# Whole-row first loads, a thinned third routing and re-placed weight splits in an attention and mixture-of-experts kernel

## The chip, the cores and the metric

The kernel runs on one core of one Trainium2 chip. The metric is device time in microseconds for one execution; lower is better. A core has TensorE (PE in the rows; PEld is its weight load), VectorE (DVE), ScalarE (ACT), GpSimd (POOL) and SyncE (SP), each with its own instruction queue that runs in order, and 16 DMA engines that all queues feed. Here SP and ACT issue the plain transfers (queues q1 and q10), GpSimd the gathers.

## The reference

Three stages follow each other; everything is float32.

```
q_pool = q.reshape(B, H, S//2, 2, D).mean(axis=3)          # B=4, H=8, S=1152, D=64
attn   = softmax(q_pool @ k.T / sqrt(D)) @ v               # 576 pooled queries per head
x      = attn.transpose(0,2,1,3).reshape(2304, 512)
logits = x @ w_gate + modality_bias[modality_id]           # 8 experts
e      = argmax(logits);  gate = softmax(logits)[e]
x      = gate * (relu(x @ w1[e]) @ w2[e])                  # top-1 expert per row
logits = x @ phi                                           # 32 slots, 4 for each of 8 experts
slots  = softmax(logits, axis=0).T @ x
out    = softmax(logits, axis=1) @ ffn_e(slots)            # a second expert network on the slots
```

## The kernel before

Attention works on 16 **pairs** of heads, p = 0 to 15; four pairs make a batch. A pair has 36 **positions** `pos`: two halves u of the queries, nine blocks c of 128 keys, two heads j. At each position PE computes a 128x288 block of scores by two matmuls (`S1` L247 and `S2` L253, on values cut into high and low parts), and ACT takes the exponential of it (`e`, L257). After every sixth position, at pos 2, 8, 14, 20, 26 and 32, stands a `group`: 12 matmuls with V (`PV`, L267), and three additions into the running sum of exponentials (`accadd`, L278 and L280, on GpSimd; in pair 15 mostly on DVE). There are three score buffers in PSUM.

Between these stands the work of other pairs. `maxpiece` (L198, L195): matmuls into `mps` whose row maximum DVE takes (L200), for the pair after this one; PSUM has three buffers for it, shared with everything small (tag `mx`). `maxred` (into `MXZ`, L207 and L209) and `maxrow` (`nps` on PE, then L218 and L221 on DVE) end it, at pos 29 and 31. `prep` (casts `KC`, `QC` on ACT, `KL`, `QL` by subtraction, copies by SP's queue) makes the operands of pair p+2. `fin0`, `fin1`, `fin2` finish a half: sums and routing logits (`sg`, `sgT`, `xr`).

When a batch is done, its **routing** is put into `queue` at pos 18 of the next pair, as a list of one-instruction steps, and the loop over positions takes one from its head: at every second position for p < 12, at every position from p = 12 on (`QSTEP`, L653). The steps are `choose` (L380 to L385: maximum and chosen expert), `gates` (L409 to L414), `place` (`ranks`: small matmuls `rp` L352 to L356; then L389 to L393; then one-hot rows, four ACT instructions (L368, L369) at a time at the groups; then `table` L362) and `count`. Routing of batches 0, 1 and 2 thus starts in pairs 4, 8 and 12. With the third batch (p = 12) there is more: `ahead.select` picks the expert of a first task of the expert stage, `fetch` gathers its weights (eight gathers into tiles that attention no longer needs), `split` cuts them into high and low parts (a cast on ACT L750, a subtraction on DVE L751), `load_x` gathers its rows, and `turn` transposes them. The list `work` holds what is placed by position; `AF2`, `5 * i + 3` and the numbers after `p == n - 1` set it. For p = 16 the fourth routing and the first matmuls of the expert stage (`hp`, L759 to L761) run.

The first pair has its own code (`first`). It needs each head's K and Q twice, on partitions 0 to 63 and 64 to 127. `twice` loads each piece by two transfers of 64 partitions: 12 from SP, 6 from ACT. A transfer waits for the landing of the one eight before it, since eight completion semaphores take turns; so ACT's fourth, fifth and sixth transfers hold ACT itself. Then come `khi` (cast, L472), `klo` (subtraction, L476), `qadd` (L465, L466), 18 maximum pieces, `maxred`, two subtractions of pair 1's `prep` (L173), and `maxrow0` (L229, L236, L241), which the first `S2` waits for.

Of the kernel before, what the change touches and what calls it, by code (L numbers as in the profile page):

```python
# [7 lines left out]
F32 = mybir.dt.float32  # L8
F32R = mybir.dt.float32r
I32 = mybir.dt.int32  # L10
AF = mybir.ActivationFunctionType
# [5 lines left out]
B, H, S, D = 4, 8, 1152, 64  # L17
HP = H // 2
SQ = S // 2
# [19 lines left out]
QSTEP = 2  # L39
# [42 lines left out]
def attention(ctx, tc, g):  # L82
    nc = tc.nc
    qT, kT, vT, wg = g["qT"], g["kT"], g["vT"], g["wg"]
# [6 lines left out]
    V = nc.vector  # L91
# [20 lines left out]
    n = len(pairs)  # L112
# [89 lines left out]
    def maxred(p, blks):  # L202
        s = st[p]
        Z = MXZ
        if min(blks) < 4:
            b0, b1 = min(blks), min(max(blks), 3) + 1
            V.reduce_max(Z[:, :, 64 + b0:64 + b1], s["mxp"][:, 0:8].rearrange("p (j b) t -> p j b t", j=2)[:, :, b0:b1], axis=AX.X)  # L207
        if 4 in blks:
            V.reduce_max(Z[:, :, 68:69], s["mxp"][:, 8:9].unsqueeze(1).to_broadcast([128, 2, 1, 3]), axis=AX.X)  # L209
# [207 lines left out]

    def in_order(r, select=None):
        choose, place, count, gates = r
        if select is None:  # L420
            return choose[:3] + gates + choose[3:] + place + count
        expert, rows = select
        place = place[:1] + count + expert + [lambda i=i: ahead.fetch(i) for i in range(2)] + place[1:]
        return choose[:3] + gates + choose[3:] + place + rows

    def first():

        b, hp = pairs[0]
        st[0] = s = dict(v=VT[0], mxp=sp.tile([128, 9, 3], F32, name="mxp"))
        operands(0)  # L430
        kx = [VT[i].rearrange("p a b c -> p (a b c)") for i in (2, 3)]
        qx = cp.tile([128, 2, 2, SQ], F32, name="qx0", tag="xr", bufs=1)
        third = lambda t: slice(t * 384, (t + 1) * 384)
        qq = [slice(0, 128), slice(128, 384)]
        q2 = [slice(0, 384), slice(384, SQ)]
        js = lambda j: slice(j * 64, (j + 1) * 64)

        def twice(eng, out, src):

            for u in range(2):  # L440
                eng.dma_start(out=out[u * 64:(u + 1) * 64], in_=src)

        twice(nc.sync, kx[0][:, third(0)], kT[b, hp, js(0), third(0)])
        for c in (qq[0], slice(128, SQ)):
            twice(nc.scalar, qx[:, 0, :, c], qT[b, hp, js(0), :, c])
        for t in (1, 2):
            twice(nc.sync, kx[0][:, third(t)], kT[b, hp, js(0), third(t)])
        twice(nc.scalar, qx[:, 1], qT[b, hp, js(1)])
        for t in range(3):
            twice(nc.sync, kx[1][:, third(t)], kT[b, hp, js(1), third(t)])  # L450
        load(1)
        load_v(0)
        P = nc.gpsimd
        P.memset(mask[64:69], 0.0)
        P.affine_select(out=mask[64:69], in_=mask[64:69], pattern=[[-1, 5], [0, 128]],
                        compare_op=ALU.not_equal, fill=-1.0, base=0, channel_multiplier=1)
        P.memset(MXZ, 0.0)
        QB0 = s["QB"] = cp.tile([128, 2, 128], F32R, name="QB0", tag="rA", bufs=1)
        P.memset(QB0.bitcast(F32), 0.0)
        P.memset(QB.bitcast(F32), 0.0)  # L460
        V.memset(KH[0][64:69].bitcast(F32), 1.0)
        qs0 = cp.tile([128, 2, SQ], F32, name="qs0", tag="rR", bufs=1)

        def qadd(ve, j, c):
            ve.tensor_add(qs0[:, j, c], qx[:, j, 0, c], qx[:, j, 1, c])  # L465
            nc.scalar.copy(QS[0][:, j, c], qs0[:, j, c])  # L466

        def ql(ve, j, c):
            ve.tensor_sub(QL[0][0:64, j, c], qs0[0:64, j, c], QS[0][0:64, j, c].bitcast(F32))  # L469

        def khi(j, t):
            nc.scalar.copy(KS[0][:, j, third(t)], kx[j][:, third(t)])  # L472

        def klo(ve, j, t):
            c = third(t)
            ve.tensor_sub(KS[0][64:128, j, c], kx[j][64:128, c], KS[0][64:128, j, c].bitcast(F32))  # L476

        wp = ps.tile([128, 512], F32, name="warm", tag="pv", bufs=2)

        def warm(k):  # L480
            for _ in range(k):
                nc.tensor.matmul(wp[:, 0:128], ident, ident, start=True, stop=True)

        warm(SWARM[0])
        khi(0, 0)
        klo(V, 0, 0)
        qadd(V, 0, qq[0])
        khi(0, 1)
        qadd(V, 0, qq[1])
        khi(0, 2)  # L490
        maxpiece(0, 0)
        klo(V, 0, 1)
        maxpiece(0, 1)
        maxpiece(0, 2)
        klo(V, 0, 2)
        for i in range(3):
            khi(1, i)
        for m in range(3, 9):
            maxpiece(0, m)
            warm(SWARM[1])  # L500
        klo(P, 1, 0)
        qadd(P, 1, qq[0])
        qadd(P, 1, qq[1])
        klo(P, 1, 1)
        klo(P, 1, 2)
        for j in range(2):
            nc.scalar.copy(KH[0][0:64, j], kx[j][0:64])
        prep1 = prep(1, P)
        for j in range(2):
            ql(P, j, q2[0])  # L510
        load(2)
        for f in prep1[:4]:
            f()
        for j in range(2):
            qadd(P, j, q2[1])
            nc.scalar.copy(QB0[:, j, j * 64:(j + 1) * 64], qs0[:, j, 512:576])
            ql(P, j, q2[1])
        return prep1, warm
# [7 lines left out]
    for m in range(9, NP0):  # L526
        maxpiece(0, m)
        warm(SWARM[2])
    maxred(0, [0, 1, 2])
    for f in prep1[4:6]:  # L530
        f()
    maxrow0(0, [(0, 256), (256, 288)])
    nc.sync.dma_start(out=wgbd[0:64, :, 0:E], in_=wg[0])
    nc.sync.dma_start(out=wgbd[64:128, :, E:2 * E], in_=wg[1])
    consts = g["route_consts"]()
# [1 line left out]
    for p in range(n + 1):  # L537
        work = {}

        def at(pos, *fs):  # L540
            work[pos] = work.get(pos, []) + list(fs)
# [21 lines left out]
        if p < n:  # L563
            if p + 1 < n:
                late = 3 if p == 0 else 0
                at(MR[0] + late, lambda: maxred(p + 1, [0, 1, 2, 3, 4]))
                at(MR[1] + late, lambda: maxrow(p + 1))
            late = 4 if p == 0 else 0
            at(FA[0] + late, lambda: fin0(p, 0))
            at(FA[1] + late, lambda: fin1(p, 0))  # L570
            if pairs[p][1]:
                at(FA[2], lambda: fin2(p, 0))
# [10 lines left out]
        if p == n - 2:  # L583
            for i in range(2, 6):
                at(AF2[i - 2], lambda i=i: ahead.fetch(i))
            for i in range(6):
                at(5 * i + 3, lambda i=i: ahead.split(i))
        if p == n - 1:
            at(0, lambda: ahead.fetch(6), lambda: ahead.load_x(0), lambda: ahead.load_x(1))
            at(10, lambda: ahead.turn(0))  # L590
            at(12, lambda: ahead.turn(1))
            at(13, ahead.gates, lambda: ahead.fetch(7))
            for i in range(6):
                at(5 * i + 3, lambda i=i: ahead.split(6 + i))
        if p == n:
            group(n - 1, 2 * NKB // GS - 1)
            assert not queue
# [47 lines left out]
        for pos, z in enumerate(units):  # L645
            if pos >= 3:
                S1(p, *z)
            S2(p, *z)
            for f in work.get(pos, []):
                f()  # L650
            if p and pos % CST == 0 and consts:
                consts.pop(0)()
            if queue and pos >= (8 if p < n - 3 else 0) and pos % (QSTEP if p < n - HP else 1) == 0 and callable(queue[0]):  # L653
                queue.pop(0)()
            if pos % (2 * GS) == LAG - 1:
                for _ in range(NHOT):
                    if queue and not callable(queue[0]):
                        queue.pop(0)[1]()
            if pos == LAG - 1 and p > 0:
                group(p - 1, 2 * NKB // GS - 1)  # L660
            elif pos >= 2 * GS and pos % (2 * GS) == LAG - 1:
                group(p, pos // (2 * GS) - 1)
            if pos == 3 and p + 3 < n:
                if p == 0:
                    load_v(2)
                load(p + 3)
# [734 lines left out]
            f()  # L1401


def moe_kernel(tc, qT, kT, vT, wg, mod, mbias, w1, w2, phi, m2w1, m2w2, out):
    nc = tc.nc
    with ExitStack() as ctx:
        gp = ctx.enter_context(tc.tile_pool(name="gp", bufs=1))
# [3 lines left out]
        keep = {**dict.fromkeys(("ident", "ones128", "si", "sel", "xidx", "axidx", "nop"), gp),  # L1411
                **dict.fromkeys(("widx", "xidx", "ntask", "C", "agt", "awidx", "neg", "acc", "sums", "nm", "lT", "m4", "nmc", "w", "siw", "rc"), gf)}
        dr = ctx.enter_context(tc.tile_pool(name="dr", bufs=1, space=DRAM))
        g = dict(qT=qT, kT=kT, vT=vT, wg=wg, w1=w1, w2=w2, phi=phi, m2w1=m2w1, m2w2=m2w2, out=out)
        g["xs"] = dr.tile([PAD + N, XW], F32, name="xs")
        g["ls"] = dr.tile([PAD + N, NSL], F32, name="ls")

# [169 lines left out]
def _layout(inputs):  # L1587
# [4 lines left out]
    a = {}  # L1592
# [10 lines left out]
    w2 = inputs["moe2_w2"].reshape(2, 4, KF, 128, DM)  # L1603
    parts = [w2[..., d0:d0 + dw].reshape(2, 4, KF * dw // 512, 512 // dw, 128, dw).transpose(0, 2, 4, 3, 1, 5).reshape(-1, 128, 2048) for d0, dw in PARTS]
    a["m2w2"] = np.concatenate(parts)
    return a


# [18 lines left out]
```

## Time and profile before

| | |
|---|---|
| median of 3 runs | 847.51 us (847.25 to 848.96) |
| profiled execution | 850.42 us, span 848.7 us from its first to its last instruction |
| PE, share of the span busy | 95% (804.7 us) |
| DVE, ACT, POOL | 68%, 55%, 63% |
| mean granted TensorE clock | 0.988 of full speed |
| attention, from the first S1 (22.76 us) to the first matmul of the expert stage | 494.8 us |

The profiled execution is one more run than the three. PE is busy nearly throughout, so what counts is where it is not, and where its clock is below full speed. A row of the timeline gives start, duration, engine, line, operation, `out<-in`, count, and in brackets how long the engine sat idle before and what ended that. A row of a stretch gives its bounds and length, then busy time (and count) of PE, PEld, DVE, ACT and POOL, the granted TensorE clock as a share of full speed (1.00 is 2.4 GHz, 0.50 is 1.2 GHz), the share of the DMA engines busy, and GB/s.

### The profile page before, as it was taken

How to read it: one execution, taken by the hardware profiler on the slowest of the kernel's cores; microseconds unless marked ns; L12 is line 12 of the kernel's file. 1: busy time of each engine (PE TensorE's matmuls, PEld its weight loads, DVE VectorE, ACT ScalarE, POOL GpSimd, SP SyncE). 2: the span in 40 equal slices, each digit the busy share in tenths (PEclk: the TensorE clock that was granted, in tenths of full speed). 3: DMA queues.
4: the chain of work that ended last, by engine and by line, in shares of the span. 5: the costliest groups of instructions: out<-in, count | busy, mean ns of one | idle time of the engine just before them, and what ended most of it. 6: DMA issues, size and time to landing. Idle time of an engine off the chain costs nothing. (4 is left out here: it accounts for less than half of the span.)

```text
span 848.7 us, 16170 instructions
## 1 busy us (share of the span) xinstructions
PE 804.7 (95%) x5808; PEld 616.1 (73%) x5808; DVE 576.0 (68%) x1180; ACT 465.1 (55%) x1106; POOL 537.3 (63%) x497
## 2 busy tenths in 40 slices
PE   4889999999999999999899999999999999999997
PEld 3657777677677676777676667788898988888446
DVE  5777777768776877877686765666576665764262
ACT  4446665657766568665377573355465555553123
POOL 5768899998888987789598842634545454441100
PEclk9999999999999999999799999999999999999999
DMA  8896649675664595566362210787786876847797
GB/s 262 199 242 154 174 137 225 144 196 145 152 168 139 120 241 151 140 159 167 99 149 79 70 57 1 220 287 252 251 288 196 312 275 248 275 160 255 277 398 225
DMA packets 58874, 163.13 MB, mean 192 GB/s; under 512 B 14682, under 2 KB 23322, under 8 KB 54682
## 3 DMA queue, kind: packets, MB, share of 16 engines
q1 hardware_dynamic: 41844, 96.42, 40.8%
q0 software_dynamic: 13760, 47.60, 16.7%
q10 hardware_dynamic: 3184, 18.02, 6.0%
q8 instruction: 47, 0.77, 0.4%
q14 instruction: 39, 0.32, 0.1%
HBM read 110.71 MB, written 10.90 MB: 143 GB/s over the span
## 5 line engine op out<-in xcount | busy, mean ns | idle before, releaser
L280 POOL TENSOR_TENSOR acc<-acc,e 128x576 f32<-128x576 f32 x214 | 313.6, 1465 | 39.7 <-ACT e L257 26.5
L257 ACT ACTIVATE e<-sc 128x288 f32<-128x288 f32 x576 | 224.2, 410 | 154.4 <-PE sc L253 132.3
L200 DVE TENSOR_REDUCE mxp<-mps 128x1 f32<-128x384 f32 x432 | 220.4, 549 | 102.2 <-PE mps L198 92.8
L247 PE MATMUL sc<-QS,KS 128*128 128x288 f32 x576 | 188.0, 334 | 4.2 <-ACT e L257 4.0
L253 PE MATMUL sc<-QL,KH 69*128 69x288 f32 x576 | 170.4, 298 | 2.2 <-DVE QL L241 1.7
L267 PE MATMUL pv<-e,V 128*64 128x288 f32 x1152 | 164.0, 421 | 0.0
L247 PEld LDWEIGHTS sc<-QS,KS 128*128 128x128 f32 x576 | 109.9, 191 | 53.9 <-issue 28.9
L198 PE MATMUL mps<-KS,QS 128*128 128x384 f32 x384 | 134.2, 354 | 13.6 <-ACT QS L466 11.2
L729 POOL DMA_INDIRECT wraw<-in_w,widx x72 | 72.9, 1012 | 108.6 <-DVE wlo L751 91.0
L267 PEld LDWEIGHTS pv<-e,V 128*64 128x64 f32 x1152 | 75.3, 138 | 64.3 <-issue 27.2
L751 DVE TENSOR_TENSOR wlo<-wraw,whi 128x512 fp32r<-128x512 f32 x144 | 95.4, 687 | 25.5 <-ACT whi L750 22.7
L253 PEld LDWEIGHTS sc<-QL,KH 69*128 69x128 f32 x576 | 109.9, 191 | 2.6 <-POOL QL L469 1.9
L750 ACT CAST whi<-wraw 128x512 fp32r<-128x512 f32 x144 | 83.9, 618 | 16.1 <-DMA wraw<-in_w,widx 11.6
L198 PEld LDWEIGHTS mps<-KS,QS 128*128 128x128 f32 x384 | 74.0, 194 | 16.8 <-ACT QS L466 11.7
L760 PE MATMUL hp<-xl,whi 128*128 128x256 f32 x288 | 80.8, 281 | 1.4 <-DVE xl L746 1.4
L759 PE MATMUL hp<-xh,whi 128*128 128x256 f32 x288 | 81.8, 284 | 0.0
L761 PE MATMUL hp<-xh,wlo 128*128 128x256 f32 x288 | 80.5, 280 | 0.0
L278 POOL TENSOR_TENSOR acc<-e 128x576 f32<-128x576 f32 x31 | 44.3, 1427 | 42.5 <-ACT e L257 42.4
L766 ACT ACTIVATE hh<-hp 128x256 fp32r<-128x256 f32 x72 | 27.6, 383 | 78.3 <-PE hp L761 65.6
L767 DVE SCALAR_TENSOR_TENSOR hl<-hp,hh 128x256 fp32r<-128x256 f32 x72 | 30.5, 423 | 44.5 <-ACT hh L766 27.2
L773 PE MATMUL yp<-whi,hh 128*128 128x512 f32 x144 | 59.6, 414 | 0.0
L760 PEld LDWEIGHTS hp<-xl,whi 128*128 128x128 f32 x288 | 54.1, 188 | 4.9 <-DVE xl L746 2.2
(363 smaller groups left out, 1243.7 us busy)
## 6 DMA issues: line engine op xcount, KB each, us to landing
mw<-in_m2w ACTq DMA_DIRECT2D x16, 1024.0 KB
mw<-in_m2w SPq DMA_DIRECT2D x16, 1024.0 KB
V<-in_vT SPq DMA_DIRECT2D x16, 576.0 KB
KX<-in_kT SPq DMA_DIRECT2D x15, 576.0 KB
QX<-in_qT SPq DMA_DIRECT2D x15, 576.0 KB
KS<-KC SPq DMA_DIRECT2D x30, 288.0 KB
KH<-KC SPq DMA_DIRECT2D x30, 288.0 KB
QS<-QC SPq DMA_DIRECT2D x60, 144.0 KB
```

Source lines behind the costliest of these rows:

```text
L198: nc.tensor.matmul(mps[:, :384], s["QS"][:, j, blk * 128:(blk + 1) * 128], s["KS"][:, j, ks], start=True, stop=True)
L200: V.reduce_max(s["mxp"][:, slot, t:t + 1], mps[:, :384], axis=AX.X)
L247: nc.tensor.matmul(sc[:, :NU], s["KS"][:, j, c * 128:(c + 1) * 128], s["QS"][:, j, u * NU:(u + 1) * NU], start=True, stop=False)
L253: nc.tensor.matmul(sc[:, :NU], s["KH"][0:69, j, c * 128:(c + 1) * 128], s["QL"][0:69, j, u * NU:(u + 1) * NU], start=False, stop=True)
L257: nc.scalar.activation(s["e", u, c][:, j], sc[:, :NU], AF.Exp, scale=SM)
L267: nc.tensor.matmul(pv[j * 64:(j + 1) * 64, :NU], s["v"][:, j, c, :], e[:, j], start=(c == 0), stop=(c == NKB - 1))
L280: eng.tensor_add(s["acc", u], s["acc", u], s["e", u, c])
L750: nc.scalar.copy(hi, x)
L751: nc.vector.tensor_sub(lo, x, hi.bitcast(F32))
L759: nc.tensor.matmul(hp, wh[:, c], xh[:, k], start=(k == 0), stop=False)
L760: nc.tensor.matmul(hp, wh[:, c], xl[:, k], start=False, stop=False)
L761: nc.tensor.matmul(hp, wl[:, c], xh[:, k], start=False, stop=(k == DM // 128 - 1))
```

## The change

- The host lays out two more arrays, `k0` and `q0`, in which each head's K and Q of the first pair stand twice. `first` loads them by five transfers of all 128 partitions: the first third of K, the rest of it, the second head's K and Q by SP, the first head's Q (now in one piece) by ACT.
- A one-element exponential (`tiny`) stands on ACT right behind its one load, with the activation table load ahead of it.
- `maxrow0` is called ahead of the two subtractions of pair 1.
- From p = 12 on the queue is served at two of three positions, and for the third batch three empty steps stand at five places; one empty step stands ahead of `place` for the others.
- `split` stands at the groups (2, 8, 14, ...); `load_x`, `turn` and `gates` of the first task stand later in pair 15, `fetch(7)` earlier, and `fin0` and `fin1` of pair 15's first half four positions later.

```diff
     def in_order(r, select=None):
         choose, place, count, gates = r
+
+        rest = [lambda: None] * 3
         if select is None:
-            return choose[:3] + gates + choose[3:] + place + count
+            return choose[:3] + gates + choose[3:] + rest[:1] + place + count
         expert, rows = select
-        place = place[:1] + count + expert + [lambda i=i: ahead.fetch(i) for i in range(2)] + place[1:]
-        return choose[:3] + gates + choose[3:] + place + rows
+        place = place[:1] + count + rest + expert + [lambda i=i: ahead.fetch(i) for i in range(2)] + place[1:]
+        return choose[:3] + rest + gates + choose[3:] + rest + place + rows[:1] + rest + rows[1:]
...
-        twice(nc.sync, kx[0][:, third(0)], kT[b, hp, js(0), third(0)])
-        for c in (qq[0], slice(128, SQ)):
-            twice(nc.scalar, qx[:, 0, :, c], qT[b, hp, js(0), :, c])
-        for t in (1, 2):
-            twice(nc.sync, kx[0][:, third(t)], kT[b, hp, js(0), third(t)])
-        twice(nc.scalar, qx[:, 1], qT[b, hp, js(1)])
-        for t in range(3):
-            twice(nc.sync, kx[1][:, third(t)], kT[b, hp, js(1), third(t)])
+        far = slice(384, S)
+        nc.sync.dma_start(out=kx[0][:, third(0)], in_=g["k0"][0][:, third(0)])
+        nc.scalar.dma_start(out=qx[:, 0], in_=g["q0"][0])
+        nc.sync.dma_start(out=kx[0][:, far], in_=g["k0"][0][:, far])
+        nc.sync.dma_start(out=kx[1], in_=g["k0"][1])
+        nc.sync.dma_start(out=qx[:, 1], in_=g["q0"][1])
+
+        tiny = sp.tile([1, 2], F32, name="tiny", bufs=1)
+        V.memset(tiny, 0.0)
+        nc.scalar.activation(tiny[:, 1:2], tiny[:, 0:1], AF.Exp)
...
     maxred(0, [0, 1, 2])
+    maxrow0(0, [(0, 256), (256, 288)])
     for f in prep1[4:6]:
         f()
-    maxrow0(0, [(0, 256), (256, 288)])
...
-            late = 4 if p == 0 else 0
+            late = 4 if p in (0, n - 1) else 0
...
-                at(5 * i + 3, lambda i=i: ahead.split(i))
+                at(6 * i + 2, lambda i=i: ahead.split(i))
...
-            at(0, lambda: ahead.fetch(6), lambda: ahead.load_x(0), lambda: ahead.load_x(1))
-            at(10, lambda: ahead.turn(0))
-            at(12, lambda: ahead.turn(1))
-            at(13, ahead.gates, lambda: ahead.fetch(7))
+            at(0, lambda: ahead.fetch(6), lambda: ahead.fetch(7))
+            at(14, lambda: ahead.load_x(0), lambda: ahead.load_x(1))
+            at(26, lambda: ahead.turn(0))
+            at(28, lambda: ahead.turn(1))
+            at(29, ahead.gates)
...
-            if queue and pos >= (8 if p < n - 3 else 0) and pos % (QSTEP if p < n - HP else 1) == 0 and callable(queue[0]):
+            if queue and pos >= (8 if p < n - 3 else 0) and (pos % QSTEP == 0 if p < n - HP else pos % 3 < 2) and callable(queue[0]):
```

Three places show the order that follows. The first is ACT's queue at the program's start (`KS` and `QS` are the first pair's operands); before:

```order
L1623 UNCONDITIONAL_BRANCH
L441 DMA qx_172<-in_qT 64x2x128 x2
L441 DMA qx_172<-in_qT 64x2x448 x2
L441 DMA qx_172<-in_qT 64x1152 x2
L472 ACT_TABLE_LOAD
L472 CAST KS_138<-V_162 128x384
L466 CAST QS_144<-qs_204 128x128
```

and now:

```order
L1623 UNCONDITIONAL_BRANCH
L440 DMA qx_172<-in_q 128x1152
L447 ACT_TABLE_LOAD
L447 ACTIVATE tiny<-tiny 1x1
L469 CAST KS_138<-V_162 128x384
L463 CAST QS_144<-qs_194 128x128
```

One transfer in place of six stands ahead of the table load, and the table load no longer stands behind a wait for data.

The second is DVE's queue in pair 12, from the subtraction of pair 14's `KL` at pos 20 (`mxp` is a maximum piece, `lg` and `sm` are the routing, `MXZ` ends the maxima); before:

```order
L173 TENSOR_TENSOR KL<-KX_150,KC 128x576
L382 TENSOR_TENSOR lg<-lg,sm 96x48
L200 TENSOR_REDUCE mxp<-mps 128x1 x2
L410 TENSOR_REDUCE sm<-ex 96x6
L200 TENSOR_REDUCE mxp<-mps 128x1
L411 TENSOR_SCALAR sm<-sm 96x6
L412 RECIPROCAL sm<-sm 96x6
L200 TENSOR_REDUCE mxp<-mps 128x1
L413 COPY xr<-sm 96x6x8
L200 TENSOR_REDUCE mxp<-mps 128x1
L383 SCALAR_TENSOR_TENSOR rtmp<-lg,wt 96x48
```

and now:

```order
L173 TENSOR_TENSOR KL<-KX_150,KC 128x576
L200 TENSOR_REDUCE mxp<-mps 128x1
L382 TENSOR_TENSOR lg<-lg,sm 96x48
L200 TENSOR_REDUCE mxp<-mps 128x1 x4
L316 TENSOR_SCALAR rs<-sgT 96x6
L317 RECIPROCAL rs<-rs 96x6
L318 TENSOR_TENSOR LG<-sgT,rs 96x3x16
L410 TENSOR_REDUCE sm<-ex 96x6
L200 TENSOR_REDUCE mxp<-mps 128x1
L207 TENSOR_REDUCE MXZ<-mxp 128x2x4
L209 TENSOR_REDUCE MXZ<-mxp 128x2
L200 TENSOR_REDUCE mxp<-mps 128x1
```

The gates (L410 to L413) have moved behind the sixth group and in part behind `MXZ`; the second half of `choose` and the ranks have moved into pair 13.

The third is DVE's queue at the end of pair 14 (L751, now L749, is a split); before:

```order
L200 TENSOR_REDUCE mxp<-mps 128x1 x2
L316 TENSOR_SCALAR rs<-sgT 96x6
L317 RECIPROCAL rs<-rs 96x6
L318 TENSOR_TENSOR LG<-sgT,rs 96x3x16
L751 TENSOR_TENSOR QL_148<-KX_151,QS_145 128x512
L207 TENSOR_REDUCE MXZ<-mxp 128x2x4
L209 TENSOR_REDUCE MXZ<-mxp 128x2
```

and now:

```order
L749 TENSOR_TENSOR QL_148<-KX_151,QS_145 128x512
L200 TENSOR_REDUCE mxp<-mps 128x1
L316 TENSOR_SCALAR rs<-sgT 96x6
L317 RECIPROCAL rs<-rs 96x6
L318 TENSOR_TENSOR LG<-sgT,rs 96x3x16
L207 TENSOR_REDUCE MXZ<-mxp 128x2x4
L209 TENSOR_REDUCE MXZ<-mxp 128x2
```

No split stands between the last routing logits and `MXZ` now; one stands at the group before it, one at the group after it.

## Rows read from the trace of the kernel before

**Rows 1.** Busy time by stretch, cut at the first S1 of pairs 0, 4, 5, 6, 12 to 15.

```profile
22.76:59.51 36.75, 31.35 (x192) 23.92 (x191) 27.02 (x61) 16.60 (x42) 25.75 (x21) 0.95 0.87 206
...
146.91:176.61 29.70, 28.51 (x195) 20.44 (x195) 22.38 (x50) 17.49 (x45) 28.29 (x31) 1.00 0.48 118
176.61:207.30 30.69, 30.65 (x217) 22.47 (x217) 22.80 (x52) 20.38 (x52) 29.24 (x27) 1.00 0.84 224
207.30:238.06 30.76, 29.84 (x205) 21.42 (x204) 24.48 (x48) 22.93 (x60) 24.48 (x18) 1.00 0.56 146
...
385.86:424.33 38.47, 35.02 (x213) 25.25 (x213) 26.42 (x57) 17.53 (x45) 27.00 (x21) 0.87 0.47 118
424.33:453.95 29.62, 28.95 (x201) 20.97 (x201) 23.27 (x53) 23.48 (x60) 27.13 (x20) 1.00 0.55 129
453.95:488.66 34.71, 31.14 (x203) 21.69 (x202) 24.11 (x50) 20.17 (x55) 28.89 (x23) 0.95 0.22 77
488.66:517.60 28.94, 27.11 (x191) 17.84 (x189) 17.87 (x27) 18.59 (x50) 13.48 (x12) 1.00 0.12 36
```

**Rows 2.** Timeline of the start: ACT up to the first matmul, and DVE's reduction L207.

```profile
0.81 7.30 ACTq L441 DMA_DIRECT2D qx<-in_qT  x6
...
8.14 1.28 ACT L472 ACT_TABLE_LOAD   x1 [8.14 <-DMA qx<-in_qT]
9.43 0.51 ACT L472 CAST KS<-V 128x384 fp32r<-128x384 f32 x1
...
11.24 1.73 PE L198 MATMUL mps<-KS,QS 128*128 128x384 f32 x3 [11.24 <-ACT QS L466]
...
22.12 0.17 DVE L207 TENSOR_REDUCE MXZ<-mxp 128x6 f32<-128x18 f32 x1
```

**Rows 3.** Busy time by 2 us: 64-partition loads, then 128-partition loads.

```profile
6.00:8.00 2.00, 0.00 (x0) 0.00 (x0) 0.00 (x0) 0.00 (x0) 0.00 (x0) 1.00 0.89 238
...
18.00:20.00 2.00, 2.00 (x15) 1.89 (x14) 2.00 (x5) 1.21 (x3) 2.00 (x3) 1.00 1.03 399
```

**Rows 4.** Timeline of PE: matmuls behind its longer idle times.

```profile
58.15 0.41 PE L195 MATMUL mps<-KC,QB 128*128 128x384 f32 x1 [2.64 <-DMA QB<-QC]
...
406.48 0.40 PE L247 MATMUL sc<-QS,KS 128*128 128x288 f32 x1 [1.46 <-ACT e L257]
...
415.31 0.53 PE L352 MATMUL rp<-oh,tri 96*96 96x48 f32 x2 [1.99 <-DVE oh L385]
...
483.70 0.70 PE L216 MATMUL nps<-ident,MXZ 128*69 128x128 f32 x2 [1.77 <-DVE MXZ L209]
...
508.17 0.44 PE L300 MATMUL sg<-acc,ones 128*32 128x288 f32 x2 [1.11 <-DVE acc L280]
```

**Rows 5.** Busy time by 2 us behind two of these idle times.

```profile
416.00:418.00 2.00, 2.00 (x13) 1.91 (x12) 0.00 (x0) 0.00 (x0) 0.45 (x1) 0.50 0.00 0
...
484.00:486.00 2.00, 2.00 (x10) 1.24 (x11) 1.50 (x3) 0.41 (x1) 1.71 (x2) 0.50 0.00 0
```

**Rows 6.** Timeline of DVE: routing steps in pair 12, and L411 after attention.

```profile
404.45 1.41 DVE L382 TENSOR_TENSOR lg<-lg,sm 96x48 f32<-96x48 f32 x1
...
407.29 1.02 DVE L411 TENSOR_SCALAR sm<-sm 96x6 f32<-96x6 f32 x1
...
528.68 0.16 DVE L411 TENSOR_SCALAR sm<-sm 96x6 f32<-96x6 f32 x1
```

**Rows 7.** Timeline of pair 12's and 14's end: ACT's gate step, DVE's split.

```profile
405.89 0.24 ACT L409 ACTIVATE ex<-lg 96x48 f32<-96x48 f32 x1 [1.76 <-DVE lg L382]
...
481.89 1.61 DVE L751 TENSOR_TENSOR QL<-KX,QS 128x512 fp32r<-128x512 f32 x1 [0.18 <-ACT QS L750]
```

**Rows 8.** Timeline: one PV group on PE; ACT's split, then the next exponential.

```profile
401.54 1.68 PE L267 MATMUL pv<-e,V 128*64 128x288 f32 x12
...
462.11 0.61 ACT L750 CAST KS<-KX 128x512 fp32r<-128x512 f32 x1
...
464.30 0.39 ACT L257 ACTIVATE e<-sc 128x288 f32<-128x288 f32 x1
```

More of the change, by code (lines that the diff above doesn't have):

```diff
@@ L435, in first @@
         q2 = [slice(0, 384), slice(384, SQ)]
[L436 to L441, printed above, removed]
-        twice(nc.sync, kx[0][:, third(0)], kT[b, hp, js(0), third(0)])
-        for c in (qq[0], slice(128, SQ)):
-            twice(nc.scalar, qx[:, 0, :, c], qT[b, hp, js(0), :, c])
-        for t in (1, 2):
-            twice(nc.sync, kx[0][:, third(t)], kT[b, hp, js(0), third(t)])
-        twice(nc.scalar, qx[:, 1], qT[b, hp, js(1)])
-        for t in range(3):
-            twice(nc.sync, kx[1][:, third(t)], kT[b, hp, js(1), third(t)])
+        far = slice(384, S)
[7 more added lines that the diff above has]
+        nc.scalar.activation(tiny[:, 1:2], tiny[:, 0:1], AF.Exp)
         load(1)
@@ L586, in attention @@
             for i in range(6):
-                at(5 * i + 3, lambda i=i: ahead.split(i))
+                at(6 * i + 2, lambda i=i: ahead.split(i))
         if p == n - 1:
-            at(0, lambda: ahead.fetch(6), lambda: ahead.load_x(0), lambda: ahead.load_x(1))
-            at(10, lambda: ahead.turn(0))
-            at(12, lambda: ahead.turn(1))
-            at(13, ahead.gates, lambda: ahead.fetch(7))
+            at(0, lambda: ahead.fetch(6), lambda: ahead.fetch(7))
[3 more added lines that the diff above has]
+            at(29, ahead.gates)
             for i in range(6):
-                at(5 * i + 3, lambda i=i: ahead.split(6 + i))
+                at(6 * i + 2, lambda i=i: ahead.split(6 + i))
         if p == n:
@@ L1401, in soft_moe, with moe_kernel @@
             f()
-def moe_kernel(tc, qT, kT, vT, wg, mod, mbias, w1, w2, phi, m2w1, m2w2, out):
+def moe_kernel(tc, qT, kT, vT, wg, mod, mbias, w1, w2, phi, m2w1, m2w2, k0, q0, out):
     nc = tc.nc
@@ L1413, in moe_kernel @@
         dr = ctx.enter_context(tc.tile_pool(name="dr", bufs=1, space=DRAM))
-        g = dict(qT=qT, kT=kT, vT=vT, wg=wg, w1=w1, w2=w2, phi=phi, m2w1=m2w1, m2w2=m2w2, out=out)
+        g = dict(qT=qT, kT=kT, vT=vT, wg=wg, w1=w1, w2=w2, phi=phi, m2w1=m2w1, m2w2=m2w2, k0=k0, q0=q0, out=out)
         g["xs"] = dr.tile([PAD + N, XW], F32, name="xs")
@@ L1605, in _layout @@
     a["m2w2"] = np.concatenate(parts)
+    a["k0"], a["q0"] = (np.stack([np.concatenate([t[j * D:(j + 1) * D]] * 2) for j in range(2)]) for t in (a["kT"][0, 0], a["qT"][0, 0]))
     return a
```

## Prediction, made before the changed kernel ran

> **What bounds the kernel now.** I read the busy times by stretch first. PE is the bound of the attention: an ordinary pair late in it takes about what its matmuls take, and pairs 5 and 4 need 30.69 and 29.70 us with a routing in them [rows 1]. Two places stand out. The first is the start: the first S1 comes at 22.76 us, and pair 0 takes 36.75 us. The second is the third routing: pair 12 takes 38.47 us, with a mean clock of 0.87, and pair 14 takes 34.71 us with 0.95, against 29.70 for pair 4, which has the same part of the first batch's routing in it [rows 1].
>
> Then the timeline of the start. ACT is held by its own six transfers for 7.30 us (from 0.81 on), then loads its table for 1.28 us, and only at 9.43 us casts the first third of K; the first matmul follows at 11.24 [rows 2]. From there on DVE works nearly without a gap on 18 maxima to the reduction at 22.12 [rows 2]. So what bounds the start is first ACT's queue, then DVE.
>
> Last the waits of PE, by the timeline. In pair 12 it sits for 1.46 us, since ACT, in order, stands at the gate's exponential behind a DVE step (1.76 us idle) [rows 4, 7]; then for 1.99 us, since the ranks need `oh` from a DVE that is behind [rows 4]. In pair 14 it waits 1.77 us for `MXZ`, ahead of which DVE runs a split of 1.61 us [rows 4, 7]; in pair 15 it waits 1.11 us for the sum of exponentials [rows 4]. Behind the longest two waits the clock stands at 0.50, which is 1.2 of 2.4 GHz [rows 5]. So a wait of 2 us costs more than 2 us. Two such places make pair 12 longer than pair 4 by 38.47 - 29.70 = 8.8 us [rows 1]: 4.4 us for each, wait and slow matmuls together.
>
> **The change, part by part.**
>
> *First loads and early table.* ACT now issues one transfer and loads its table while data are under way. What is left ahead of the first matmul is the landing of the first third of K (0.20 MB) and of the first head's Q (0.59 MB, in one piece, where a sixth of it sufficed), then cast, DVE's subtraction and addition, and the cast of Q, which took 11.24 - 9.43 = 1.8 us [rows 2]. The two loads share the engines with each other and with the rest of K (0.39 MB). Rates from rows: 238 GB/s for pieces on 64 partitions, 399 GB/s for rows of 128 [rows 3]. If only the 0.79 MB go first, at 399 GB/s, they need 2.0 us; if all 1.18 MB must go first at 238 GB/s, 5.0 us. I take 2 us as the time before a transfer moves anything (an estimate: in ACT's row the issue starts at 0.81, and one of its six issues takes 7.30 / 6 = 1.2 us) [rows 2]. So the first matmul comes between 2 + 2.0 + 1.8 = 5.8 and 2 + 5.0 + 1.8 = 8.8 us, 2.4 to 5.4 us earlier. I take 7.2, or 4.0 us, in the middle: the pieces are now 128-partition rows, but Q lands later than it needed to.
>
> The Trainium skill (SBUF — State Buffer, "Can I just issue two DMAs to hit both halves?") says that two transfers to 64 partitions each serialize, and that one over all 128 reaches every port. The two rates in rows 3 agree with that; by it alone the gain would be the 5.4 us. It also says (DMA: Bandwidth & Descriptors, "Issuing engines are not separate DMA queues") that ACT's and SP's transfers interleave on the same engines, so a second issuing queue adds no rate; that speaks for the lower end, 2.4 us. No row shows the two kinds together.
>
> Does the rest follow? From the first matmul to 22.12 DVE has its work in a row, so the end moves along, if the second head's K and Q are there in time. They are 1.18 MB more, 3 us at 399 GB/s, and ACT and GpSimd come to them only behind the first head's work. SP too is free earlier: it issues four transfers, not twelve, ahead of pair 1's loads. In pair 0 the longest wait, 2.64 us at 58.15 for the copy of `QB` [rows 4], is one for SP's queue; all that is in that queue starts from casts that move by the same 4 us. So pair 0 keeps its 36.75 us.
>
> *`maxrow0` ahead of two subtractions.* The first `S2` comes earlier, but the subtractions then stand ahead of the next maxima, whose PSUM buffers PE needs after three pieces. It exchanges one wait for another: I take 0, between a gain and a loss of 1.5, the size of the common waits in rows 4.
>
> *Thinned routing, pair 12.* Choose now ends at pos 21, the gate's exponential stands at pos 27, and the rest of `choose` and the ranks move into pair 13. Both waits of pair 12 lose their cause: ACT no longer stands at a step that DVE has just begun, and `oh` is made six positions ahead of the ranks. Pair 12 then has the steps of pair 4, so I take 29.6 for 38.47: a gain of 8.9. Bounds: 28.5 (no wait at all; the matmuls of pair 4 take 28.51 [rows 1]) and 34.1 (one place of 4.4 us stays).
>
> *Pair 13* now holds what pair 5 holds, choose's end, ranks and some of `place`, so 30.7 [rows 1], and the choice of the expert, its two gathers and, at pos 30 to 34, `place` beside `maxrow`: I add 1.0 for a wait there. 31.7 for 29.62: a loss of 2.1. Bounds 30.7 and 35.
>
> *Pair 14* gets the one-hot steps at all six groups, like pair 6 (30.76, [rows 1]), but no maxima for a pair after the next, so six matmuls fewer, 0.2 us each by estimate: 29.5 for 34.71, a gain of 5.2. The split that stood ahead of `MXZ` is at the groups before and behind it. A split on ACT with four one-hot steps takes 464.30 - 462.11 = 2.2 us [rows 8]; PE's group of 12 matmuls covers 1.68 of it [rows 8], and three positions that need no new score buffer cover the rest. Bounds 28.5 and 33.
>
> *Pair 15* loses the wait of 1.11 and gets two matmuls of the selection (about 0.6): 28.4 for 28.94. The gathers of rows at pos 14 have twelve of 36 positions, some 9 us of 28.94, to land ahead of `turn`; nothing else waits on GpSimd, which is busy 13.48 of 28.94 us there [rows 1].
>
> *The one empty step in batches 0 and 1* moves the ranks by two positions in pairs 5 and 9, where PE has no longer wait: nothing.
>
> Sum: 4.0 + 0 + 8.9 - 2.1 + 5.2 + 0.5 = 16.5 us. Against the profiled execution, 850.42 us, that gives 833.9; the median of the runs is 2.9 lower, at 847.51, so the forecast is **831 us**.
>
> **The rivals.**
>
> *A stall moves on with the work.* DVE's work is not less, only spread. A small step beside a GpSimd addition takes 1.02 us in pair 12 and 0.16 later, with GpSimd idle [rows 6]. Pair 13's last positions now hold four steps of `place`, the maxima and `maxrow`. If PE waits 2 us there, the clock falls as in rows 5, and one place of 4.4 us comes back: 835. The Trainium skill (SBUF — State Buffer, "Who interferes with whom") has DVE and GpSimd take a shared pair of ports by turns, the later one blocked for the whole instruction; by that rule thinning takes nothing from these steps, and this rival has the stronger hand. The rows of L411 agree.
>
> *The start is not won.* If Q and K land together late, or if SP's queue, and not the casts, sets the pace of pair 0, the wait at 58.15 grows by what the start gains. About 0.5 us is left of 4.0: 834.5.
>
> *Slower: ACT falls behind in pair 14.* At each of six groups ACT has the 2.2 us burst ahead of the next exponential. If its overrun leaves PE waiting long enough for the clock to fall, each costs about 4.4 us, 26 us in all: 831 + 26 = 857. It decides when PE loses 16.5 / 6 = 2.8 us at every group. Against it: pair 6 has the one-hot bursts at groups and casts beside them, and is idle for 0.92 us in all (30.76 - 29.84) [rows 1].
>
> *Nothing comes of it.* The waits go, but others of the same size stand in their place from pair 12 to 15, and the start is given back: within 0.2% of 847.5.
>
> **How the numbers follow.** Forecast 0.60, a stall that moves 0.17, a start not won 0.14, slower 0.05, nothing 0.04. 0.2% (1.7 us) is about what a measurement of this kernel can tell from no change. Faster 0.91, same 0.04, slower 0.05. The low end: the start at its bound (5.4) and pairs 12 to 15 at 28.5 + 30.7 + 28.5 + 28.0 = 115.7 for 131.7, 16.0: 847.5 - 21.4 = 826. The high end takes in both middle rivals together, 831 + 4.4 + 3.5 = 839.
>
> **What would show it.** ACT's table load before 4 us and the first matmul near 7 us; L207 near 18 and pair 0's first S1 near 18.5; pair 0 still at some 36.7 us. Pair 12 near 29.6 us at a clock of 1.00, ranks in pair 13 with no wait ahead of them, no wait for `MXZ` at the end of pair 14. The prediction is wrong if pair 0 grows by what the start gives, if a stretch at clock 0.50 stands in pairs 13 to 15, or if score matmuls wait for ACT behind the groups of pair 14.

## The result, and the profile after

The changed kernel takes **834.74 us** in the median of 4 runs (833.8 to 836.65) where the kernel before takes 847.84 beside it (847.25 to 848.96): a ratio of 0.9847, interval 0.9826 to 0.9867. That is 13.1 us less, where 16.5 were forecast. The profiled execution is at the median, 834.64 us, with a span of 832.9.

The busy time by stretch, cut at the first S1 of pairs 0, 4, 5, 6, 9 and 12 to 15, as in [rows 1]:

```profile
18.62:53.84 35.22, 31.95 (x192) 24.96 (x191) 28.29 (x61) 16.50 (x42) 24.09 (x21) 0.90 0.89 220
141.29:170.99 29.70, 28.51 (x196) 20.43 (x195) 22.40 (x50) 17.49 (x45) 28.29 (x31) 1.00 0.48 118
170.99:202.02 31.03, 30.57 (x217) 22.47 (x217) 22.91 (x52) 20.35 (x52) 29.58 (x27) 1.00 0.83 221
202.02:232.74 30.72, 29.80 (x205) 21.39 (x204) 24.48 (x48) 22.92 (x60) 24.47 (x18) 1.00 0.56 146
290.64:322.48 31.84, 30.61 (x217) 22.50 (x217) 25.54 (x53) 20.31 (x52) 25.52 (x18) 1.00 0.80 215
381.74:411.07 29.33, 28.54 (x196) 20.51 (x195) 22.39 (x48) 17.72 (x46) 26.22 (x20) 1.00 0.47 113
411.07:443.85 32.78, 31.45 (x220) 22.73 (x219) 26.06 (x60) 17.40 (x43) 25.62 (x19) 1.00 0.59 151
443.85:474.53 30.68, 29.61 (x199) 20.59 (x198) 24.84 (x47) 26.43 (x71) 28.84 (x21) 1.00 0.22 69
474.53:501.99 27.46, 27.30 (x195) 18.26 (x193) 20.49 (x33) 19.14 (x50) 18.60 (x16) 1.00 0.20 60
```

For the third batch the three empty steps stand at four places, as the diff has it, and not at five. Pair 12 is now an ordinary pair at full clock, and no stretch of pairs 12 to 15 is at half clock any more. Pair 13 is longer than pair 5, which holds the same steps of the first routing. The cut between pairs 14 and 15 isn't at quite the same matmul as before, so the two are read as a sum: 58.14 us for 63.63.

The timeline of the start, which answers to [rows 2], ACT, PE and DVE:

```profile
1.24 1.28 ACT L447 ACT_TABLE_LOAD   x1 [1.24 <-PEq L1614]
...
5.29 0.51 ACT L469 CAST KS<-V 128x384 fp32r<-128x384 f32 x1 [2.55 <-DMA V<-in_k]
...
7.10 1.73 PE L198 MATMUL mps<-KS,QS 128*128 128x384 f32 x3 [7.10 <-ACT QS L463]
...
17.98 0.17 DVE L207 TENSOR_REDUCE MXZ<-mxp 128x6 f32<-128x18 f32 x1
```

The first matmul comes at 7.10 for 11.24, and the reduction L207 at 17.98 for 22.12: the 4.1 us pass through DVE's row of maxima undiminished. ACT now waits for data and not for its own queue.

PE's matmuls behind its longer waits, which answer to [rows 4]:

```profile
23.46 0.66 PE L198 MATMUL mps<-KS,QS 128*128 128x384 f32 x1 [2.70 <-DVE mxp L200]
...
317.53 0.40 PE L247 MATMUL sc<-QS,KS 128*128 128x288 f32 x1 [1.23 <-ACT e L257]
...
417.26 0.44 PE L198 MATMUL mps<-KS,QS 128*128 128x384 f32 x1 [0.77 <-DVE mxp L200]
...
435.09 0.44 PE L300 MATMUL sg<-acc,ones 128*32 128x288 f32 x2 [0.54 <-DVE mxp L200]
```

The four long waits of pairs 12, 14 and 15 are gone, and so is that for `QB` at the end of pair 0. New are 1.23 us in pair 9 and two short ones in pair 13. The 2.70 us in the first positions of pair 0 stand in place of a shorter wait there; before:

```profile
25.06 0.37 PE L253 MATMUL sc<-QL,KH 69*128 69x288 f32 x1 [1.66 <-DVE QL L241]
```

Behind the longer one the clock is at 0.50, and pair 0's mean is 0.90 for 0.95:

```profile
24.00:26.00 2.00, 2.00 (x9) 2.00 (x8) 1.74 (x4) 0.66 (x2) 0.88 (x1) 0.50 0.82 186
```

### The profile page after: what moved, and what is told of

It reads as the page before. It is cut to its first block, busy times and chain, and to the rows that moved or that the text cites. A ratio compares the mean times of both kernels' runs of the same rounds, so it can differ in the third digit from the quotient of the medians.

```text
span 832.9 us, 16154 instructions
## 1 busy us (share of the span) xinstructions
PE 799.8 (96%) x5808; PEld 613.3 (74%) x5808; DVE 581.1 (70%) x1181; ACT 465.9 (56%) x1107; POOL 539.6 (65%) x497
## 5 line engine op out<-in xcount | busy, mean ns | idle before, releaser
L267 PE MATMUL pv<-e,V 128*64 128x288 f32 x1152 | 160.9, 415 | 0.0
L749 DVE TENSOR_TENSOR wlo<-wraw,whi 128x512 fp32r<-128x512 f32 x144 | 95.6, 688 | 26.9 <-ACT whi L748 24.4
```

Of the source, the lines that this page charges most:

```text
L267: nc.tensor.matmul(pv[j * 64:(j + 1) * 64, :NU], s["v"][:, j, c, :], e[:, j], start=(c == 0), stop=(c == NKB - 1))
L749: nc.vector.tensor_sub(lo, x, hi.bitcast(F32))
```

## The experiments

Ratios are to the kernel before on the same chip. before_again, b_start, a_maxold and a_norest shared one set of its runs (848.8 us), c_kl, a_oldloads, a_notab and a_split5 another (849.0), the other four a third (846.0).

**A second profile of the kernel before.**

> The kernel before, unchanged, for a second profile. In the first one the execution took 850.42 us, 2.6 above the median of 847.84, while the changed kernel's profiled execution (834.64) stands at its median. Theory: the 2.6 us are a longer stall in pairs 12 to 15, whose waits throw the clock to 0.50 by an amount that differs from execution to execution; then this profile shows about 847.8 us, pairs 12 to 15 near 129 us in place of 131.7, and the start and pair 0 as before (22.8 and 36.7 us). Rival one: the 2.6 us lie in pair 0, in the wait of 2.64 us for the copy of QB, which is then missing here (pair 0 near 34 us). Rival two: the profiled execution of this kernel is always that long, so it shows 850.4 again with the same stretches.

Its profiled execution takes 845.95 us, 4.5 less than the first; the median of ten runs is 847.36, ratio 0.9984 (0.9968 to 1.0), as it must be for the same kernel. The first S1 is 1.0 us later (23.76), but pair 0 takes 33.63 us for 36.75, with no wait for `QB`, and pair 12 35.55 for 38.47. Pairs 1 to 11, 13 to 15 and the expert stage agree to some 0.5 us in all. Pair 12, two of its stretches of 2 us, and PE's two waits in it:

```profile
383.70:419.25 35.55, 31.98 (x213) 23.02 (x213) 26.59 (x57) 17.57 (x45) 27.05 (x21) 0.95 0.50 127
...
407.00:409.00 2.00, 2.00 (x18) 1.55 (x15) 1.45 (x3) 0.83 (x3) 1.04 (x2) 1.00 0.37 104
...
415.00:417.00 2.00, 2.00 (x11) 1.03 (x12) 1.64 (x5) 0.41 (x1) 0.81 (x1) 0.50 0.00 0
```

```profile
404.33 0.40 PE L247 MATMUL sc<-QS,KS 128*128 128x288 f32 x1 [1.47 <-ACT e L257]
...
411.67 0.34 PE L352 MATMUL rp<-oh,tri 96*96 96x48 f32 x2 [2.10 <-DVE oh L385]
```

The waits are those of [rows 4], 1.47 and 2.10 for 1.46 and 1.99. What differs is the clock: here it falls behind the second wait alone, there it fell behind both, and the mean over the pair is 0.95 for 0.87. The stretch behind the first wait in the first profile, for the row 407.00:409.00 here:

```profile
410.00:412.00 2.00, 2.00 (x9) 1.24 (x6) 0.04 (x1) 0.35 (x1) 0.00 (x0) 0.56 0.65 197
```

So theory and rival one each hold half: the execution from which the forecast took its terms had 2.9 us more than this one in pair 12 and 3.1 more in pair 0.

**The start alone.** The kernel before with `first` of the changed kernel and `maxrow0` moved; queue, splits and pair 15 as before.

> The kernel before with the new start alone (five loads of whole rows, early table, maxima's row ahead of the two subtractions). Theory: the start is worth what the changed kernel's trace shows up to pair 1, 59.51 - 53.84 = 5.7 us: 842.1 us, with pair 0 at 35.2 us and no wait for QB. Rival one: only the first loads' 4.1 us are the change's, and pair 0's other 1.5 us are chance: 843.7, pair 0 at 36.7. Rival two, the recorded one: pair 0 grows by what the start gives: about 847.

Ratio 0.9935 (0.9912 to 0.9958), 843.89 us: by the ratio 5.5 us, between 3.6 and 7.5. Its trace has the first S1 at 18.96, pair 0 at 35.15 us, no wait for `QB`; pair 1 starts at 54.11. Against the two profiles of before (59.51, 57.39) that is 5.4 and 3.3 us. Pair 12 takes 37.06 here, the third value for the same instructions: the new start does nothing for it. The start is won; rival two falls, and between the others the spread of the kernel before decides nothing.

**Old loads, new table.** The twelve loads again, on SP for K (not shown) and on ACT for Q, the small exponential ahead of them:

```diff
-        nc.scalar.dma_start(out=qx[:, 0], in_=g["q0"][0])
         ...
         nc.scalar.activation(tiny[:, 1:2], tiny[:, 0:1], AF.Exp)
+        for c in (qq[0], slice(128, SQ)):
+            twice(nc.scalar, qx[:, 0, :, c], qT[b, hp, js(0), :, c])
+        twice(nc.scalar, qx[:, 1], qT[b, hp, js(1)])
```

> The changed kernel with the twelve loads of 64 partitions again, six of them on ACT's queue, and the early table kept ahead of them on ACT. Theory: the start's gain is the loads'. ACT's six issues hold it for about 7.3 us as before, now behind the table, so the first cast stands near 9.5 us, the first matmul near 11.3, the first S1 near 22.8: 838.8, 4.1 us more than the changed kernel. Rival: the gain is the early table's, 1.28 us of load off the path, and the rest comes of ACT's shorter issue only in part; then the first matmul is near 10 us and the time near 837.5.

Ratio 0.9895 (0.9869 to 0.9921), 840.76 us. ACT at the start:

```profile
0.80 1.28 ACT L440 ACT_TABLE_LOAD   x1 [0.80 <-PEq L1622]
...
2.35 7.79 ACTq L446 DMA_DIRECT2D qx<-in_qT  x4
10.24 0.51 ACT L477 CAST KS<-V 128x384 fp32r<-128x384 f32 x1 [7.94 <-DMA qx<-in_qT]
```

With the table loaded at 0.80 the first cast still stands behind ACT's six transfers, at 10.24, and the first S1 at 24.25, both later than the theory gave (9.5 and 22.8): ACT's sixth transfer, which waits for an earlier landing, is issued at 9.64 where before it was at 7.62. The gain of the start is that of the loads, all of it: the theory holds. Which property of the loads it is, fewer transfers or whole rows, this run does not separate.

**New loads, no exponential.** The three lines of `tiny` taken out.

> The changed kernel without the small exponential, so the table is loaded with the first cast of K. Theory: with one issue on its queue ACT is free from 1.2 us on, and the load of the table needs no data, so it runs there at 1.2 us all the same, 4 us ahead of the first cast: no difference, 834.7. Rival: the load waits with the cast for K, and the first matmul comes 1.28 us later, at 8.4 us: 836.0.

```profile
1.25 1.28 ACT L466 ACT_TABLE_LOAD   x1 [1.25 <-PEq L1611]
5.42 0.51 ACT L466 CAST KS<-V 128x384 fp32r<-128x384 f32 x1 [2.89 <-DMA V<-in_k]
```

The table is loaded at 1.25 us without it, 4.2 us ahead of the cast whose line it carries; the first matmul comes at 7.22, the first S1 at 18.75. In this start `tiny` does nothing. The time, 837.79 us at 0.9853 (0.9819 to 0.9888), is 3 us above the forecast, and its profiled execution has 2.7 us of that in pair 5, where the wait of 0.46 us is 1.58 this time, with the clock at 0.50 behind it:

```profile
198.69 0.40 PE L247 MATMUL sc<-QS,KS 128*128 128x288 f32 x1 [1.58 <-ACT e L257]
```

```profile
200.00:202.00 2.00, 2.00 (x9) 1.04 (x10) 1.96 (x4) 1.38 (x5) 1.84 (x3) 0.50 0.13 47
```

Why the wait is longer there isn't settled.

**The row of maxima back behind the subtractions.**

> The changed kernel with the row of maxima behind the two subtractions again, as before. Theory: the new place makes PE wait 2.70 us for the maxima where it waited 1.66 for QL, so the old place gives back 1.0 us: 833.7, second S1 behind the first three near 22.7 us instead of 23.9, and no wait for QB, since SP's queue does not depend on it. Rival: the new place is what took the wait for QB away; then a wait near 2.6 us stands there again near 54 us, and the time is 1.5 us longer, 836.2. No difference to be measured in the time (within 1.5 us) leaves it to the profile.

835.04 us, ratio 0.9829 (0.9805 to 0.9853). PE waits 2.71 us at 22.97 for `QL` in place of 2.70 for a maximum, and pair 1 starts at 54.38 for 53.84; no wait for `QB`. My theory falls, the rival too: one wait is exchanged for another of its size, as the prediction had it.

**The subtractions spread.** Without the empty step, and `prep1[4]` and `prep1[5]` not ahead of pair 0's loop but at its positions 1 and 2:

```diff
-    for f in prep1[4:6]:
-        f()
...
         if p == 0:
+            at(1, prep1[4])
+            at(2, prep1[5])
```

> The changed kernel without the empty step, and with pair 1's two subtractions not in a row ahead of the maxima but one each behind the positions 1 and 2 of pair 0. Theory: the 1.85 us that PE waits at 23.4 us (2.70 in the changed kernel) go, and with them part of the 5 us at half clock behind them; pair 0 takes 33 to 33.5 us in place of 34.75, so 831.0 against the 832.66 of the kernel without the empty step. Rival: DVE has the same work up to the next row of maxima, so the wait only moves behind it, and pair 0 stays at 34.7: 832.7.

835.71 us, ratio 0.9836 (0.9808 to 0.9864), and pair 0 takes 38.53 us: longer than both expected. (The interval overlaps that of the kernel without the empty step, 0.9784 to 0.9832; the trace decides.) The wait at 23.4 breaks into two, 0.87 and 1.32 us, and a new one stands behind; SP's queue, then PE:

```profile
31.67 1.16 SPq L149 DMA_DIRECT2D KS<-KL  x2
```

```profile
35.34 0.52 PE L198 MATMUL mps<-KS,QS 128*128 128x384 f32 x1 [2.56 <-DMA KS<-KL]
```

The copies of `KL` now stand 4 us later on SP (27.80 in the changed kernel), behind four small loads, and pair 1's first maxima wait for them. DVE's order was only half of what the step sets.

**QB's copies first.** In `qc`, the two copies of `QB` ahead of the four of `QS`.

> The changed kernel without the empty step, and with each pair's two copies of QB issued ahead of the four of QS on SP's queue instead of behind them. In eight profiled executions so far PE waited 0 to 3.5 us for QB near the end of pair 0 (2.64 in the kernel before, 3.46 in a_split5, none in five), whatever was changed. Theory: QB lands late because its copies stand last in a queue that is still moving the loads issued before; ahead of QS's they land 3.5 us or more earlier, so no wait for QB, pair 0 at 34.8 us, and the runs lie closer together: median 832, highest below 833.5. Rival: the queue is late for everything behind those loads, so the wait moves to QS or KS: the same median and spread as the kernel without the empty step alone, 832.7, up to 834.5.

830.99 us, ratio 0.9816 (0.9801 to 0.9831), beside 830.46 for the same kernel without this edit: no difference, as the rival has it for the time. The five runs lie closer together (828.61 to 831.38, for 828.85 to 833.24), which five runs can't settle. And none of the other profiles of that set has a wait for `QB`, so what causes it stays open. Over all profiles of the study it is 0 to 3.46 us, whatever was changed.

**DVE without GpSimd in pair 12.** `accadd` of the kernel before leaves out all but the first addition of pair 12's two sums:

```diff
-        elif c > 1:
+        elif c > 1 and p != n - 4:
```

> The kernel before without 14 of pair 12's 16 additions of exponentials on GpSimd (the sums of that pair are then wrong; DVE, ACT and PE keep all their steps). Theory: pair 12's two waits come of DVE's small routing steps, 1.0 to 1.4 us each beside a GpSimd addition and 0.2 without; so those steps take 0.2 us here, the waits of 1.46 us for the exponential and 2.0 for oh go, and pair 12 takes 29.5 us at a clock of 1.00 in place of 35.6 to 38.5: about 841. Rival: the queue of routing steps itself is too long, with one step at every position; then the waits stay above 1 us each and pair 12 above 33 us.

The sums change the fourth batch's routing, so the total (907.6 us) says nothing; pair 12 is read alone. DVE's two steps of [rows 6], PE's wait for `oh`, and the stretches:

```profile
402.94 0.20 DVE L382 TENSOR_TENSOR lg<-lg,sm 96x48 f32<-96x48 f32 x1
...
404.59 0.32 DVE L411 TENSOR_SCALAR sm<-sm 96x6 f32<-96x6 f32 x1
```

```profile
410.00 0.34 PE L352 MATMUL rp<-oh,tri 96*96 96x48 f32 x2 [0.82 <-DVE oh L385]
```

```profile
385.04:419.06 34.02, 33.20 (x213) 24.00 (x213) 21.39 (x57) 17.60 (x45) 8.99 (x8) 0.90 0.53 133
...
412.00:414.00 2.00, 2.00 (x9) 1.64 (x11) 1.06 (x3) 0.41 (x1) 0.00 (x0) 0.50 0.05 18
414.00:416.00 2.00, 2.00 (x10) 1.03 (x12) 1.59 (x5) 0.41 (x1) 0.00 (x0) 0.50 0.00 0
```

The steps shrink from 1.41 and 1.02 to 0.20 and 0.32 us, the wait for the exponential is gone, that for `oh` is 0.82 for 2.0. So GpSimd's additions are the cause of the first wait and of more than half of the second: shown. The Trainium skill (SBUF — State Buffer, "Who interferes with whom") has a DVE instruction with two inputs in SBUF exclude a GpSimd instruction that reads there, and a reduction never; these durations agree: L382 subtracts one tile from another, and the reduction L410 takes 0.19 us in both profiles. Yet pair 12 takes 34.0 us, not the 29.5 of the theory: behind the remaining 0.82 us the clock is at 0.50 again. The wait's own length is the smaller part of what this place costs: 0.82 of the 4.7 us by which the pair is longer than in the changed kernel. No run takes the thinning apart into the service at two of three positions and the empty steps.

**Pair 14's splits.** At every fifth position again (`at(5 * i + 3, ...)`), pair 15's left at the groups.

> The changed kernel with pair 14's weight splits at every fifth position again (3, 8, 13, ...), all else kept. Theory: the split at position 28, 1.6 us on DVE ahead of MXZ, was the cause of the 1.77 us wait and of the half clock behind it, so both return: pairs 14 and 15 together 62 us in place of 58.1, 838.7. Rival: with the routing thinned out DVE is no longer behind at that place, and the split is covered: 834.7, no wait for MXZ above 0.8 us.

837.77 us, ratio 0.9862 (0.9837 to 0.9887). Pairs 14 and 15 take 61.33 us for 58.14, and PE's wait is back:

```profile
475.98 0.44 PE L216 MATMUL nps<-ident,MXZ 128*69 128x128 f32 x2 [1.55 <-DVE MXZ L209]
```

Behind it the half clock is back as well:

```profile
478.00:480.00 2.00, 2.00 (x9) 0.86 (x6) 0.00 (x0) 0.82 (x2) 1.55 (x3) 0.50 0.00 0
```

So 3.2 of the 5.5 us come of the splits' place; the theory holds, with a little less than it gave. The other 2.3 us, most of them in pair 15, no run takes apart. (The profiled execution, 842.47 us, also had the longest wait for `QB`, 3.46 us.)

**The empty step of batches 0 and 1**, taken out, twice:

```diff
-            return choose[:3] + gates + choose[3:] + rest[:1] + place + count
+            return choose[:3] + gates + choose[3:] + place + count
```

> The changed kernel without the one empty step ahead of place in batches 0 and 1 (the prediction: worth nothing). Theory: this step is what makes PE wait 0.46 us in pair 5 and 1.23 in pair 9 for an exponential behind the selection on ACT, since rdf comes two positions later; without it pair 5 is back at 30.7 and pair 9 at 30.6, 1.6 us less: 833.1. Rival: these waits come of other timing between DVE and GpSimd, started earlier by the new start; then pairs 5 and 9 stay at 31.0 and 31.8: 834.7.

> The changed kernel without the empty step, beside the changed kernel on one chip. Theory: it takes 1.6 us less, 0.33 of it in pair 5 and 1.20 in pair 9, as in its first trace. Rival: the 2 us between the two medians so far come from different chips and times, and side by side they differ by less than 0.8 us.

> The changed kernel, unchanged. Theory: again near 834.7 us, pairs 5 and 9 at 31.0 and 31.8, pair 12 at 29.3 and pair 13 at 32.8 as in its first trace to 0.1 us, since no wait above 1 us is left there, and only pair 0 differs by the wait for QB. Rival: pair 12 or 13 differ by over 1 us between executions, as pair 12 does in the kernel before (38.5, 35.6 and 37.1 us in three).

832.66 us at 0.9808 (0.9784 to 0.9832) the first time; then 830.46 at 0.9817 (0.9797 to 0.9836), beside 831.78 at 0.9839 (0.9823 to 0.9854) for the changed kernel. The intervals overlap, so the totals alone don't settle 1.3 us; the traces do. Pairs 5 and 9 of a_norest:

```profile
170.70:201.41 30.71, 30.66 (x218) 22.50 (x218) 22.85 (x52) 20.65 (x52) 29.27 (x27) 1.00 0.84 224
288.50:319.14 30.64, 30.64 (x219) 22.45 (x217) 25.24 (x53) 19.19 (x49) 25.83 (x18) 1.00 0.83 224
```

In norest_again they take 30.68 and 30.64, in after_again 31.04 and 31.86. The row in pair 9 of the changed kernel that makes the wait, on ACT:

```profile
315.41 0.35 ACT L368 ACTIVATE far<-i,rdf 96x72 f32<-96x72 f32 x1 [1.86 <-DVE rdf L393]
```

ACT, in order, stands for 1.86 us at a selection step whose input DVE has only just made, and the next exponential and PE's score matmul stand behind it. after_again also shows that the changed kernel's pairs repeat: 1 to 15 agree with its first profile to 0.1 us each (pair 12 29.33 both times), and only pair 0 differs, 34.07 for 35.22. (The expert stage is 3.7 us shorter there, 327.25 us, on a chip on which the kernel before is faster too.)

## Why the prediction was right, and where 3.4 us went

The forecast of the sign, of the four places and of their mechanisms held. Its terms, the first profile of before against that of after, and the second profile of before against the same:

| term, us won | forecast | first profile | second profile |
|---|---|---|---|
| up to the first S1 | 4.0 | 4.1 | 5.1 |
| pair 0 | 0 | 1.5 | -1.6 |
| pairs 5 and 9 | 0 | -1.6 | -1.6 |
| pair 12 | 8.9 | 9.1 | 6.2 |
| pair 13 | -2.1 | -3.2 | -3.2 |
| pairs 14 and 15 | 5.7 | 5.5 | 5.6 |
| all else | 0 | 0.2 | 0.8 |
| sum | 16.5 | 15.8 | 11.3 |

**The step that failed** is the last: "the median of the runs is 2.9 lower". The sum was made against one execution that was 2.9 us above the median, and the 2.9 were then taken off the result too, as if the changed kernel's execution carried them as well. The second profile shows where they lay: in pair 12, whose clock fell twice, and in pair 0's wait for `QB`. The changed kernel has no such place in pair 12, and its profiled execution is at its own median. The mean of the two last columns, 13.5, is close to the 13.1 us measured; so pair 12 was worth 6.2 to 9.1 us, depending on the execution it is held against, and the 8.9 of the forecast is near the upper end.

**Two terms were mis-sized.** Pair 13 lost 3.2 us, not 2.1: its matmuls take 31.45 us, where pair 5's, which the term was taken from, take 30.65, and 1.3 us of waits stand beside them. Of these 0.77 us are behind an `oh` step of 1.31 us on DVE:

```profile
415.43 1.31 DVE L385 TENSOR_TENSOR oh<-rtmp,sm 96x48 f32<-96x48 f32 x1
```

It is the first rival's place, at a fraction of its price, since the clock stayed at 1.00. And the one empty step was costed at nothing since "PE has no longer wait" there; it costs 1.6 us, as two positions later ACT has come to the selection before DVE has its input ready. In a_notab's execution the same place in pair 5 cost 2.7 us more, by a longer wait and the half clock behind it. That no wait stood there before was no cover. The two misses come to 2.7 us; in the first column the 1.5 us of pair 0, which lie within its spread between executions, hide more than half of that.

**What held by the wrong reason.** Of the start's two edits only the loads count; that the table is early follows from ACT's short queue, not from `tiny`. Their size was right, 7.10 us for a forecast of 7.2, and the first third of K does land between the bounds, at 5.29 us. But the 1.2 us that the sum took as the length of one issue aren't that. Before, each of ACT's six issues takes 0.49 to 0.82 us, 3.7 us in all; the rest of the 7.30 us ACT stands until earlier transfers have landed, longest ahead of the sixth. Its fifth and sixth, with nothing between them:

```profile
4.30 0.59 ACTq L441 DMA_DIRECT2D qx<-in_qT  x1
```

```profile
7.62 0.49 ACTq L441 DMA_DIRECT2D qx<-in_qT  x1
```

The fifth waits for the landing of the first third of K, so that was there by 4.30 us, 5.1 us ahead of its cast, and earlier than in the changed kernel; the first piece of Q was there by 5.36, when SP issues a transfer that waits for it. What held the first cast was ACT's queue of six transfers and not the rate of the pieces; no run leaves the pieces as they were with fewer of them on ACT, so what the whole rows add stays open.

The second rival, pair 0 growing by what the start gives, is refuted by the trace of after and by b_start for most of the gain, but against the second profile of before alone pair 0 grew by 1.6 of 5.1 us. b_nopool12 has the old start too, with the first S1 at 23.89 us and pair 0 at 34.76. So pair 0 takes 33.63 to 36.75 us with the old start (three profiles) and 34.07 to 35.22 with the new one (after, after_again, b_start), and the forecast of no change holds within that spread. ACT's bursts in pair 14 (the slower rival) left nothing: 1.1 us of idle time in the pair, at full clock.

The best kernel of the study is the changed one without the empty step, 830.46 us by the median. Its lead of 1.3 us over the changed kernel on the same chip is within the intervals; it rests on the traces of pairs 5 and 9.

## What to carry to other kernels

Where a place with half clock carries a term, take a second profile's worth of care: with the same waits pair 12 took 35.6, 37.1 and 38.5 us in three executions, so give the term as a range, and do not subtract the profile's excess over the median a second time. An empty step or a later position is not free on an engine that runs in order: look at what the moved step's input waits for at the new place. And a step that is moved for one engine's sake takes its DMAs with it to another place in a queue; look there before counting the gain. A merged row of transfers is not the engine's issue time: part of it can be waits between them.

## What the runs showed of the hardware

- The clock falls in some executions and not in others behind waits of the same length: behind 1.46 us in pair 12 it was at 0.56 over 2 us in one execution and at 1.00 in two, behind 0.82 us in pair 12 (b_nopool12) it fell to 0.50, behind 0.77 in pair 13 of the changed kernel it did not.
- ACT's table load (1.28 us) does not wait for the data of the instruction that needs it: it ran at 1.25 us, the cast at 5.42.
- An issue holds ACT for 0.40 us in the changed kernel (0.81 to 1.21) and for 0.49 to 0.82 us in the kernel before. The longer part of the 7.79 us that four transfers take in a_oldloads is waits for the landing of earlier ones: the four issues take 2.2 us.
- DVE steps of 0.20 and 0.32 us (L382, L411 in b_nopool12) take 1.41 and 1.02 beside GpSimd's additions. Thinning the queue leaves them at 0.96 and 1.12 in the changed kernel; it takes PE's wait away.
